# The last 512 queries of a transformer block's forward half in two chunks of 256, with the PSUM banks shared out anew

## Chip, cores and metric

One NeuronCore of a Trainium2 chip. The metric is device time in microseconds (us) of one launch. The engines are written PE (matrix products, "TensorE"), ACT (ScalarE), DVE (VectorE), POOL (GpSimd) and SP (which here only issues DMAs). Matrix products go into PSUM, eight banks of 128 partitions by 512 float32; a tile of 128x1024 float32 takes two banks.

## The reference, cut to what matters

A block of adaptive layer norm, attention with 32 heads of 16 channels, and a two-layer network with squared ReLU, over 2048 tokens of width 512. The kernel must give the block's output and its gradients by nine inputs.

```
mod = (_silu(c) @ w_mod).reshape(c.shape[0], 6, 1, -1)       # sa, ca, ga, sb, cb, gb
h = _layernorm(x) * (1 + ca) + sa
x = x + ga * _A_ref(h, A_wqkv, A_wo)                          # attention, S = 2048, H = 32, Dh = 16
h = _layernorm(x) * (1 + cb) + sb
x = x + gb * _B_ref(h, B_w1, B_b1, B_w2, B_b2)                # (relu(h @ w1 + b1)**2) @ w2 + b2, F = 1792
...
_out, _vjp = jax.vjp(_f, A_x, A_wqkv, A_wo, B_w1, B_b1, B_w2, B_b2, c, w_mod)
_grads = _vjp(grad_out)
```

## The kernel before, in words

There are four stages. A short preparation makes the first projections. The **forward** stage (`fscore`, `fpv`, lines 567 to 610) runs the attention. A stage **between** (`late_finish`, `last_chunk`, lines 650 to 668 and 1233 to 1490) does the dense work of the last queries. The **backward** stage (lines 1594 to 1760) runs the attention's gradient, and a tail makes the projections' gradients. The change touches the forward stage and the stage between.

**Forward.** The 2048 queries are four chunks of 512. The loop goes over 512 units (`funits`): for each chunk, for each of 8 groups of 4 heads, for each of 16 key tiles of 128 keys. One unit makes the scores of 4 heads (line 576: four PE products of 32 rows each, in four row groups of the array), two exponentials on ACT (line 578, each 128x1024 from a score tile of two banks), and, two units later, the products with the values (line 592: four products of 32 columns in four column groups, all into one bank `oacc`). PSUM holds three score tiles (six banks), `oacc`, and one bank `pm` for everything else.

**Dense work beside it.** When a chunk's 128 units are over, `ffinish` starts the generator `dense_chunk` for it: the output projection `wo`, the second layer norm, w1 (line 410), the first part of the gradient (w2 transposed, line 424), the products back through w1 (line 446), the network's output through w2 (line 500) and through `wo` transposed (line 532). It is advanced by `step` (line 1119), once a unit, beside the next chunk's attention; every `yield` ends a unit's share, most often four products of 512 columns. Each product lands in the one bank `pm` and is taken out by DVE. Weight gradients are "chains" (`add_chain`, line 226; the queue is `dwq`): four products, a copy by DVE into one of four `part` tiles (line 251), and a DMA that adds it to a partial sum in DRAM, issued on POOL's queue (line 255). A unit that makes no product of its own gets two idle products into `oacc` (`steady`, line 615), which add zero.

**Between.** The last chunk has no attention to hide under. After the last unit, `late_finish` completes its attention output, and `last_chunk` does its dense work alone, 512 queries at a time, with ACT and DVE sharing the evictions, the transposes on PE (line 1322), and the final sum of every weight gradient (line 237), for which the partial sums are fetched by SP's queue and the results stored by ACT's. The weights w1 (transposed) and w2 are loaded again for it, and the head rows, keys and gradients that the backward stage starts with come in as well (`head_loads`).

**Order.** All five engines stand in a hand-written order: an engine executes what the loops record, in that order, and waits in place. A recorded `later(k, ...)` is put out k units (in the stage between: k ticks) later, at the start of a unit.

## Time and profile before

| | |
|---|---|
| three runs | 2475.92, 2488.13, 2494.58 us; median 2488.13 |
| span of the profiled execution | 2501.3 us |
| first to last exponential of the forward stage | 41.2 to 996.3 us of the span |
| first exponential of the backward stage | 1115.66 us |
| exponentials of the forward stage (line 578) | 1024, 941.9 us busy |

The span is that of one execution under the profiler; it lies 13 us (0.5%) above the median of the three runs. Matmuls are pipelined in the array, so their time of about 0.38 us each overlaps with that of their neighbours; what counts for PE is how far apart they start. A group of instructions is written as engine, line, output<-inputs and shape; a tile's number is left out.

### The profile page before, as it was taken

How to read it: one execution, taken by the hardware profiler on the slowest of the kernel's cores; microseconds unless marked ns; L12 is line 12 of the kernel's file. 1: busy time of each engine (PE TensorE's matmuls, PEld its weight loads, DVE VectorE, ACT ScalarE, POOL GpSimd, SP SyncE). 2: the span in 40 equal slices, each digit the busy share in tenths (PEclk: the TensorE clock that was granted, in tenths of full speed). 3: DMA queues.
4: the chain of work that ended last, by engine and by line, in shares of the span. 5: the costliest groups of instructions: out<-in, count | busy, mean ns of one | idle time of the engine just before them, and what ended most of it. 6: DMA issues, size and time to landing. Idle time of an engine off the chain costs nothing.

```text
span 2501.3 us, 49888 instructions
## 1 busy us (share of the span) xinstructions
PE 2324.0 (93%) x18948; PEld 783.4 (31%) x19036; DVE 1837.7 (73%) x2377; ACT 2303.7 (92%) x3560; POOL 488.0 (20%) x661
## 2 busy tenths in 40 slices
PE   8899899989998998999999999999999999999989
PEld 3232233223332333443223323233232323332344
DVE  6555354455435444579989999999999999999965
ACT  7999999999998999539999999999999999999944
POOL 2111223323533453110111101111011110110100
PEclk9999999999998999999999999999999999999999
DMA  4468463258546865979999999999999999999984
GB/s 146 130 167 176 144 150 97 88 166 142 98 95 142 151 131 110 256 200 196 201 192 206 199 198 202 196 204 203 205 205 198 205 202 199 200 198 214 201 253 133
DMA packets 1189503, 437.70 MB, mean 175 GB/s; under 512 B 1065867, under 2 KB 1160521, under 8 KB 1188878
## 3 DMA queue, kind: packets, MB, share of 16 engines
q1 hardware_dynamic: 1152414, 389.35, 79.0%
q0 software_dynamic: 19872, 27.09, 6.5%
q10 hardware_dynamic: 16976, 18.07, 2.9%
q8 instruction: 149, 2.44, 0.4%
q14 instruction: 92, 0.75, 0.1%
HBM read 98.30 MB, written 70.80 MB: 68 GB/s over the span
## 4 chain that ended last, share of the span: by engine, by line
ACT 40%; PE 38%; issue 8%; DVE 7%; DMA 3%; SPq 1%; ACTq 1%; POOL 0%; DVEq 0%; another core or an unknown queue 0%; POOLq 0%
ACT E_u L1600 24%; ACT ET L578 12%; PE dqacc L1681 4%; PE psST L576 3%; PE psS_A L1594 3%; PE accVK L1654 2%; PE pm L233 2%; ACT dsT L1760 2%; PE psS_B L1594 2%; PE pdh L1858 2%; PE oacc L592 2%; PE psS_C L1594 2%; PE pwq L1892 2%; PE pm L500 2%; PE pm L410 2%
## 5 line engine op out<-in xcount | busy, mean ns | idle before, releaser
L1616 DVE TENSOR_TENSOR dS_u<-psD_u,E_u 128x1024 bf16<-128x1024 f32 x1024 | 1185.9, 1218 | 77.1 <-PE psD_u L1614 30.2
L578 ACT ACTIVATE ET<-psST 128x1024 bf16<-128x1024 f32 x1024 | 941.9, 1242 | 16.6 <-PE psST L576 16.3
L1600 ACT ACTIVATE E_u<-psS_A 128x512 bf16<-128x512 f32 x768 | 509.9, 664 | 10.8 <-PE psS_C L1594 8.5
L1600 ACT ACTIVATE E_u<-psS_B 128x512 bf16<-128x512 f32 x768 | 503.2, 655 | 10.8 <-DMA dsT<-dS_u 2.7
L1614 PE MATMUL psD_u<-iv,ido 32*128 32x512 bf16 x2048 | 409.1, 388 | 1.5 <-DVE dS_u L1616 1.3
L576 PE MATMUL psST<-qt_sb,kt_sb 32*128 32x512 bf16 x2048 | 313.8, 386 | 48.0 <-ACT ET L578 41.0
L1600 ACT ACTIVATE E_u<-psS_C 128x512 bf16<-128x512 f32 x512 | 334.3, 653 | 3.1 <-PE psS_B L1594 1.1
L1594 PE MATMUL psS_B<-ik,iq 32*128 32x512 bf16 x768 | 296.1, 386 | 11.7 <-ACT E_u L1600 4.4
L1594 PE MATMUL psS_A<-ik,iq 32*128 32x512 bf16 x768 | 294.5, 383 | 11.0 <-DVE dwlast L237 1.0
L1699 POOL TENSOR_TENSOR dQacc<-dQacc,dqtmp 128x512 f32<-128x512 f32 x64 | 81.2, 1268 | 858.8 <-ACT dqtmp L1694 797.4
L1594 PEld LDWEIGHTS <-iq 32*128 32x128 bf16 x2048 | 129.7, 91 | 313.9 <-issue 296.9
L1654 PE MATMUL accVK<-dS_u,qz 128*32 128x512 bf16 x2048 | 213.5, 388 | 0.5 <-PE psD_u L1614 0.2
L592 PE MATMUL oacc<-ET,vaug 128*32 128x512 bf16 x2048 | 207.0, 394 | 3.9 <-DVE ostage L596 3.9
L1663 PE MATMUL accVK<-E_u,dOs_tok 128*16 128x512 bf16 x2048 | 204.5, 388 | 0.0
L1594 PE MATMUL psS_C<-ik,iq 32*128 32x512 bf16 x512 | 194.2, 379 | 4.5
L576 PEld LDWEIGHTS <-kt_sb 32*128 32x128 bf16 x2048 | 84.3, 91 | 328.2 <-issue 306.5
L1681 PE MATMUL dqacc<-dsT,KS_tok 128*32 128x512 bf16 x2048 | 145.7, 382 | 18.8 <-DMA dsT<-dS_u 5.0
L1760 ACT ACTIVATE dsT<-ptT 128x1024 bf16<-128x1024 bf16 x128 | 144.1, 1126 | 13.1 <-PE ptT L1644 12.2
L251 DVE COPY part<-pm 128x512 f32<-128x512 f32 (+2 forms) x106 | 65.2, 615 | 121.9 <-PE pm L233 111.8
L1614 PEld LDWEIGHTS <-ido 32*128 32x128 bf16 x2048 | 105.2, 91 | 101.3 <-issue 94.9
L1654 PEld LDWEIGHTS <-qz 128*32 128x32 bf16 x2048 | 58.5, 94 | 178.0 <-issue 162.9
L1699 POOL TENSOR_TENSOR dQst<-dQacc,dqtmp 128x512 bf16<-128x512 f32 x32 | 40.6, 1270 | 266.1 <-ACT dqtmp L1694 266.1
(415 smaller groups left out, 2688.7 us busy)
## 6 DMA issues: line engine op xcount, KB each, us to landing
p_st<-part POOLq DMA_DIRECT2D x36, 256.0 KB, 4.6
kt_sb<-qkT_st POOLq DMA_DIRECT2D x124, 64.0 KB, 3.0
wA<-in_B_w_dram SPq DMA_DIRECT2D x28, 256.0 KB
wB<-w1T_st SPq DMA_DIRECT2D x21, 256.0 KB
wA<-w2T_st SPq DMA_DIRECT2D x21, 256.0 KB
wB<-in_B_w_dram SPq DMA_DIRECT2D x21, 256.0 KB
p_st<-part POOLq DMA_DIRECT2D x28, 192.0 KB, 4.6
p_st<-part SPq DMA_DIRECT2D x18, 256.0 KB
```

The source lines that it names most:

```text
L576: PE.matmul(ps[:, hi, :], kt_sb[r:r + 32, kt * P:(kt + 1) * P], qt_sb[r:r + 32, :], start=True, stop=True, tile_position=(r, 0))
L578: ACT.activation(ET[:, 2 * pair:2 * pair + 2, :], ps[:], AF.Exp, scale=SCALE)
L592: PE.matmul(oacc[32 * hq:32 * hq + 32, :], lhsT, ET[:, hq, :], start=(kt == 0), stop=(kt == TT - 1), tile_position=(0, 32 * hq), skip_grou ...
L1594: PE.matmul(psS[:], st["q"][r:r + 32, qt * P:(qt + 1) * P], st["k"][r:r + 32, kc * 512:kc * 512 + 512], start=True, stop=True, tile_positi ...
L1600: ACT.activation(bst[u][0][:, hq, :], sst.pop((u, hq))[:], AF.Exp, scale=SCALE)
L1614: PE.matmul(psD[:, hi, :], st["do"][r:r + 32, qt * P:(qt + 1) * P], st["v"][r:r + 32, kc * 512:kc * 512 + 512], start=True, stop=True, til ...
L1616: DVE.tensor_tensor(dS_u[:, 2 * pair:2 * pair + 2, :], psD[:], E_u[:, 2 * pair:2 * pair + 2, :], ALU.mult)
L1654: PE.matmul(cur["vk"][32 * hq:32 * hq + 32, :], hst[hg]["qz"][:, qt, hq, :], bst[u][1][:, hq, :], start=(qt == 0), stop=False, tile_positi ...
L1663: PE.matmul(acc[32 * hq:32 * hq + DH, :], dOs_tok[:, qt, (hg * 4 + hq) * DH:(hg * 4 + hq + 1) * DH], E_u[:, hq, :], start=False, stop=(qt ...
L1681: PE.matmul(acc[32 * hq:32 * hq + 32, :], KS_tok[:, kc * 4 + kt, h * DH:h * DH + 32], tT[:, :, hq * 4 + kt, :], start=(kt == 0), stop=(kt ...
L1699: POOL.tensor_tensor(dst2, dst, tmp[:], ALU.add)
L1760: ACT.activation(dst, pt[:], AF.Identity)
```

## The change

The queries are cut into five chunks: three of four tiles of 128 queries, and two of two tiles (`CH`). A unit of a short chunk covers two key tiles for 256 queries, so there are still 512 units and 1024 exponentials of the same size; its score and value products have 256 columns and are twice as many. The dense work of the fourth chunk (256 queries) now runs in `dense_chunk` under the fifth's attention; only the fifth's is left to `last_chunk`. In the last 128 units `step` is called twice a unit. The products through w1 and w2 of a short chunk are 256 wide, and a `yield` stands after every second of them.

PSUM is shared out anew: two score tiles (four banks), `oacc`, two banks `pm`, and one bank `pg` for the long sums of lines 446 and 500 (14 products each), between which chains can now run. In a unit the first pair's scores come first, then the value products of two units before, then the second pair's scores. `steady` is left out as well where the generator ran without a product. The last two head groups, before the last one, are finished after the loop. The loads of a head group's keys and queries (`fload`) stand 12 units ahead of the group, and 7 units ahead, two a unit, behind a short chunk's group of 8 units.

```diff
     TT = n // P
     QC = n // 512
     NS = -(-FC // 3)
+    CH = [(4 * i, 4) for i in range(QC - 1)] + [(TT - 4, 2), (TT - 2, 2)]
+    NC = len(CH)
...
             else:
                 POOL.tensor_tensor(racc[:, j, :], racc[:, j, :], src, ALU.add)
 
-        open_group = [False]
+        def group():
+            products[0] += 1
+            return pools["mm"].tile([P, 512], F32, name="pg", tag="pg", bufs=1)
+
...
                     acc = mm()
-                for ti in range(4):
-                    PE.matmul(acc[:, 0:w], lhs(ti), rhs(ti), start=(ti == 0), stop=(ti == 3))
-                if c == QC - 1:
+                nt = CH[c][1]
+                for ti in range(nt):
+                    PE.matmul(acc[:, 0:w], lhs(ti), rhs(ti), start=(ti == 0), stop=(ti == nt - 1))
+                if c == NC - 1:
                     late = idx >= FC + 4 * NS
...
+            ts = slice(t0, t0 + nt)
+            end = c == NC - 1
+            L = dict(begun)
+            begun.clear()
+            if not L:
+                L["w1"] = load_wA(w1_src, 6)
+                L["g"] = chunk_tile("g_c", "g_c", nt)
+                sp(L["g"], g_dram[:, ts, :])
+            if not end:
+                L["w1T"] = load_wB(w1T_st[:], 20) if nt == 4 else load_wB(w1T_st[:], 6, 0.5)
...
-            for ti in range(4):
-                later(5 + ti, scaled, ti)
+            for ti in range(nt):
+                later(5 + ti if nt == 4 else 1 + ti, scaled, ti)
                 later(24 + 2 * ti, sums, ti)
             return L
 
...
-            ts = slice(4 * c, 4 * c + 4)
+            t0, nt = CH[c]
+            W = nt * P
+            every = 4 // nt
+            ts = slice(t0, t0 + nt)
...
...
-                    PE.matmul(pz[:], w1_nat[:, ic, fc * P:(fc + 1) * P], h2T[:, :, ic, :],
+                    PE.matmul(pz[:, 0:W], w1_nat[:, ic, fc * P:(fc + 1) * P], h2T[:, :, ic, :],
                               start=(ic == 0), stop=(ic == DC - 1))
-                DVE.tensor_scalar(rT[:, fc, :], pz[:], b1col[:, fc:fc + 1], 0.0, ALU.add, ALU.max)
+                DVE.tensor_scalar(rT[:, fc, :], pz[:, 0:W], b1col[:, fc:fc + 1], 0.0, ALU.add, ALU.max)
                 DVE.tensor_tensor(sT[:, fc, :], rT[:, fc, :], rT[:, fc, :], ALU.mult)
                 if fc % 3 == 2 or fc == FC - 1:
                     f0 = fc // 3 * 3
                     to_tokens("s", sT, f0, fc + 1)
-                yield 0
+                if fc % every == every - 1:
+                    yield 0
...
             rest = []
-            for ti in range(4):
-                t = 4 * c + ti
-                pdh = mm()
+            for ti in range(nt):
+                t = t0 + ti
+                pdh = group()
                 for fc in range(FC):
                     PE.matmul(pdh[:], dzT[:, fc, ti * P:(ti + 1) * P], w1T[:, fc, :],
                               start=(fc == 0), stop=(fc == FC - 1))
                     if fc == 3 and rest:
                         rest.pop()()
...
-        funits = [(qc, hg, kt) for qc in range(QC) for hg in range(HG) for kt in range(TT)]
+            for ti in range(nt):
+                later(lag + more, sp, d_st[:, (t0 + ti) * P:(t0 + ti + 1) * P], dltT[H * ti:H * ti + H, :])
+
+        funits = [(ch, hg, j) for ch in range(NC) for hg in range(HG) for j in range(TT * CH[ch][1] // 4)]
+        first = {}
+        for u, (ch, hg, j) in enumerate(funits):
+            if j == 0 and u > 0:
+                short = CH[funits[u - 1][0]][1] < 4
+                first.setdefault(u - (7 if short else 12), []).append((ch, hg, 2 if short else 1))
...
-        def fscore(u):
-            qc, hg, kt = funits[u]
-            qt_sb, kt_sb = fh[qc, hg]
-            ET = ework.tile([P, 4, 512], BF, name="ET", tag="ET")
-            fe[u] = ET
-            for pair in range(2):
-                ps = pools["s"].tile([P, 2, 512], F32, name="psST", tag="psST")
+            fh[c, hg] = (qt_sb, kt_sb)
+
+        def fscore(u, pair):
+            c, hg, j = funits[u]
+            nk = 4 // CH[c][1]
+            W = 512 // nk
+            qt_sb, kt_sb = fh[c, hg]
+            if pair == 0:
+                fe[u] = ework.tile([P, 4, 512], BF, name="ET", tag="ET")
+            ET = fe[u]
+            ps = pools["s"].tile([P, 2, 512], F32, name="psST", tag="psST")
+            for k in range(nk):
+                kt = j * nk + k
                 for hi in range(2):
                     r = 32 * (2 * pair + hi)
-                    PE.matmul(ps[:, hi, :], kt_sb[r:r + 32, kt * P:(kt + 1) * P], qt_sb[r:r + 32, :],
+                    PE.matmul(ps[:, hi, k * W:(k + 1) * W], kt_sb[r:r + 32, kt * P:(kt + 1) * P], qt_sb[r:r + 32, 0:W],
                               start=True, stop=True, tile_position=(r, 0))
-                ACT.activation(ET[:, 2 * pair:2 * pair + 2, :], ps[:], AF.Exp, scale=SCALE)
+            ACT.activation(ET[:, 2 * pair:2 * pair + 2, :], ps[:], AF.Exp, scale=SCALE)
 
...
-            qc, hg, kt = funits[u]
-            if kt == 0:
+            c, hg, j = funits[u]
+            nt = CH[c][1]
+            nk = 4 // nt
+            W = nt * P
...
                 if hg == 0:
-                    fcur["rr"] = ework.tile([H, 512], F32, name="rrows", tag="rrows", bufs=1)
-                    fcur["ou"] = ework.tile([P, 4, HG, P], BF, name="O_un", tag="O_un", bufs=1)
+                    if CH[c - 1][1] == nt and nt == 2:
+                        fcur["rr"], fcur["ou"] = fcur["next"]
+                    else:
+                        rr = ework.tile([H, 512], F32, name="rrows", tag="rrows", bufs=1)
+                        ou = ework.tile([P, 4, HG, P], BF, name="O_un", tag="O_un", bufs=1)
+                        fcur["rr"], fcur["ou"] = rr[:, 0:W], ou[:, 0:nt]
+                        fcur["next"] = rr[:, 256:512], ou[:, 2:4]
             oacc = fcur["o"]
             ET = fe.pop(u)
-            for hq in range(4):
-                h = hg * 4 + hq
-                lhsT = vaug[:, kt].rearrange("p h c -> p (h c)")[:, h * (DH + 1):h * (DH + 1) + 32]
-                PE.matmul(oacc[32 * hq:32 * hq + 32, :], lhsT, ET[:, hq, :],
-                          start=(kt == 0), stop=(kt == TT - 1), tile_position=(0, 32 * hq), skip_group_check=True)
-            if kt == TT - 1:
-                ostage = ework.tile([P, 512], F32, name="ostage", tag="ostage", bufs=1)
-                DVE.tensor_copy(ostage[:], oacc[:])
-                obf = ework.tile([P, 512], BF, name="obf", tag="obf", bufs=2)
-                if u == NF - 1:
-                    fcur["last"] = ostage
-                    return
-                if hg == HG - 1:
...
-                    POOL.tensor_copy(obf[:], ostage[:])
+            for k in range(nk):
+                kt = j * nk + k
                 for hq in range(4):
                     h = hg * 4 + hq
-                    later(2, sp, fcur["rr"][h:h + 1, :], ostage[32 * hq + 16:32 * hq + 17, :])
-                later(3, sp, fcur["ou"][:, :, hg, :], obf[:], True)
+                    lhsT = vaug[:, kt].rearrange("p h c -> p (h c)")[:, h * (DH + 1):h * (DH + 1) + 32]
+                    PE.matmul(oacc[32 * hq:32 * hq + 32, 0:W], lhsT, ET[:, hq, k * W:(k + 1) * W],
+                              start=(kt == 0), stop=(kt == TT - 1), tile_position=(0, 32 * hq), skip_group_check=True)
+            if kt == TT - 1:
+                if c == NC - 1 and hg >= HG - 2:
+                    last = ework.tile([P, 256], F32, name="olast", tag="obf", bufs=2)
+                    DVE.tensor_copy(last[:], oacc[:, 0:W])
+                    fcur["last", hg - HG + 2] = last
...
 
         def step(u):
             nonlocal wait, turn
-            ripe = dwq and not open_group[0] and u >= dwq[0][0]
-            if wait > 0 or not dense:
-                wait = max(0, wait - 1)
+            ripe = dwq and u >= dwq[0][0]
+            if u < wait or not dense:
                 if ripe:
                     next_chain()
                 return
...
                 dense.pop(0)
                 run_due(True)
                 if not fqueue:
-                    loads["L"] = chunk_loads(QC - 1)
-            else:
-                wait = w
-
-        fqueue = list(range(QC - 1))
+                    loads["L"] = chunk_loads(NC - 1)
+            elif w > 0:
+                wait = u + w + 1
+
+        fqueue = list(range(NC - 1))
...
-            pools["s"] = ph2.enter_context(tc.tile_pool(name="psS", bufs=3, space=bass.MemoryType.PSUM))
+            pools["s"] = ph2.enter_context(tc.tile_pool(name="psS", bufs=2, space=bass.MemoryType.PSUM))
...
-            pools["mm"] = ph2.enter_context(tc.tile_pool(name="psM", bufs=1, space=bass.MemoryType.PSUM))
+            pools["mm"] = ph2.enter_context(tc.tile_pool(name="psM", bufs=2, space=bass.MemoryType.PSUM))
...
                 fh[0, 0] = (qts[0], kts[0])
                 for u in range(NF + 2):
                     unit[0] = u
                     run_due()
+                    count = products[0]
+                    fast = u >= NF - TT * HG
                     if u < NF:
-                        if funits[u][2] == 4 and u + TT < NF:
-                            fload(*funits[u + TT][0:2])
-                        fscore(u)
+                        for args in first.pop(u, ()):
+                            fload(*args)
+                        fscore(u, 0)
                     if 2 <= u:
                         fpv(u - 2)
+                    if u < NF:
+                        fscore(u, 1)
                     if u % 4 == 2 and u // 4 < len(stages):
                         later_stage(stages[u // 4])
                     if u % 4 == 0 and 18 <= u // 4 < 32:
                         turn_weights(u // 4 - 18)
-                    count, begun_group = products[0], open_group[0]
                     for f, args in plan.pop(u, ()):
                         f(*args)
+                    worked = len(dense) > 0 and u >= wait
                     if u < NF - 4:
-                        step(u)
+                        for _ in range(2 if fast else 1):
+                            step(u)
                     elif dwq and u >= NF - 2:
                         next_chain()
-                    if products[0] == count and not (begun_group or open_group[0]):
+                    if products[0] == count and not worked:
                         steady(u - 2)
-                    if u >= NF - 7 and "L" in loads and "O" not in loads["L"]:
+                    if u >= NF - 8 and "L" in loads and "O" not in loads["L"]:
                         early_finish()
                     if u == NF:
                         tiny = wk.tile([P, 1], F32, name="tiny", tag="tiny", bufs=1)
...
             ACT.activation(dst, onesf[:, 0:1].to_broadcast([P, n]), AF.Identity, scale=value)
 
         def last_chunk(O_c, L, w1T, w2T):
-            c = QC - 1
-            ts = slice(4 * c, 4 * c + 4)
+            c = NC - 1
+            t0, nt = CH[c]
```

The rest of the diff carries the number of tiles `nt` of a chunk through the tile shapes, loops and slices of `chunk_loads`, `dense_chunk`, `attn_grad`, `store_grad`, `early_finish`, `late_finish`, `ffinish` and `last_chunk` (whose layer norm is now done in one half instead of two), and moves hooks in `last_chunk` accordingly.

## Prediction

> **What bounds the kernel now.** I read the page first: busy time by slices, then the costliest groups.

> ```profile
> span 2501.3 us, 49888 instructions
> ...
> PE   8899899989998998999999999999999999999989
> ...
> ACT  7999999999998999539999999999999999999944
> ...
> L578 ACT ACTIVATE ET<-psST 128x1024 bf16<-128x1024 f32 x1024 | 941.9, 1242 | 16.6 <-PE psST L576 16.3
> ```

> ACT is full in the first 16 slices, the forward stage, apart from 16.3 us in which it waited for scores; then comes a hole, the stage between. 941.9 us over 1024 exponentials is 0.92 us each; ends follow each other at 0.917, so ACT's floor is 1.835 us a unit, 939.5 us in all. With the 16 idle that is the 955.1 us from 41.2 to 996.3. So the forward stage is bound by ACT, and PE's nines there say little. How much room PE has is read from its timeline, in units with a dense product:

> ```profile
> 876.29 0.40 PE L592 MATMUL oacc<-ET,vaug 128*32 128x512 bf16 x4
> 876.63 1.04 PE L424 MATMUL pm<-gfT,wA 128*128 128x512 bf16 x4
> 877.60 0.39 PE L576 MATMUL psST<-qt_sb,kt_sb 32*128 32x512 bf16 x4
> 877.92 0.40 PE L592 MATMUL oacc<-ET,vaug 128*32 128x512 bf16 x4
> 878.52 1.02 PE L424 MATMUL pm<-gfT,wA 128*128 128x512 bf16 x4 [0.20 <-DVE rT L427]
> 879.48 0.39 PE L576 MATMUL psST<-qt_sb,kt_sb 32*128 32x512 bf16 x4
> ```

> Four score products start together and cost as much as one: the next kind of product starts 0.32 us after them (877.60 to 877.92), the one behind the value products likewise 0.32 to 0.34 after those, and four dense products take 0.96 (878.52 to 879.48). That is 1.60 us of 1.835; the 0.2 wait for the single bank `pm` fits in too. From the starts in the trace: products of one kind follow each other at 0.215 us with 512 columns, 0.161 with 384, 0.108 with 256 and 0.055 with 128, and a change of kind (32-row, 32-column or full array) adds 0.10.

> Last, the stage between, 119.4 us from 996.3 to 1115.7, cut at its loops (head, w1, w2 transposed, the long sums, tail):

> ```profile
> core 0: us, PE busy (x) PEld busy (x) DVE busy (x) ACT busy (x) POOL busy (x), PEclk, DMA share, GB/s
> 996.30:1016.90 20.60, 15.75 (x93) 7.05 (x93) 13.92 (x34) 11.81 (x23) 7.41 (x9) 0.96 0.95 234
> 1016.90:1045.20 28.30, 26.40 (x158) 12.72 (x160) 13.35 (x27) 17.10 (x28) 1.70 (x2) 0.97 1.03 268
> 1045.20:1070.50 25.30, 24.72 (x168) 13.73 (x168) 16.67 (x42) 11.02 (x18) 2.96 (x15) 1.00 0.82 250
> 1070.50:1107.90 37.40, 37.24 (x193) 16.56 (x194) 30.40 (x71) 11.79 (x25) 0.00 (x0) 1.00 0.79 213
> 1107.90:1115.70 7.80, 6.69 (x30) 2.38 (x29) 4.84 (x9) 0.64 (x2) 0.48 (x1) 1.00 0.70 229
> ```

> PE is busy in 110.8 of the 119.4 us, so PE bounds this stage; but the DMA engines move 238 GB/s meanwhile, 28.4 MB.

> **The first 384 units.** With two score tiles the pairs are split: scores, values, scores, so a quad's 0.32 us is paid twice. A unit costs PE 0.95 us (0.315 + 0.32 + 0.315) before dense work. I counted the products of each unit in the order of the built program. 204 units carry four products of 512 columns: 0.95 + 0.96 = 1.91 us, above ACT's 1.835. The other 180 stay below (mean 0.52 dense, 1.47 us) and cost nothing while ACT covers them. Added: 204 x 0.075 = 15.3 us, 720 instead of 704.6.

> The change adds a wait: the second pair needs the tile that the previous unit's second exponential leaves, and behind it on PE stand the dense products and the next unit's first pair, for which ACT waits. By the rows a tile's round is 0.05 from the end of an exponential to the scores, 0.385 for these, 0.10 to ACT, and at least 1.02 for the exponential (its shortest), 1.56 us: shorter than 1.835, so two tiles suffice unless PE is late. The longest way round, over the dense products and both tiles, is 0.315 + 0.96 + 0.385 + 0.10 + 1.02 + 0.917 + 0.05 = 3.75 us for two units, 1.87 each: below PE's own 1.91. Ends for this part: 10 us if coupling is kinder, 25 if the added waits on DVE come on top.

> **The last 128 units.** Two steps a unit, and PE's fixed 0.95 remains (eight products of 256 columns in place of four of 512: same columns; that 256-wide products of one row group follow without a gap is taken from the 0.108 of the full array; a further 0.10 for each would be 0.3 a unit). Units 384 to 507, dense time with the switch: 41 units of 1.7 us or more, mean 1.82, so 2.77 each, 113.6 us; 29 of mean 1.46, 69.8; 18 of mean 1.00, 35.1; 36 under ACT's floor, 66.1. Sum 284.5 us against 124 x 1.835 = 227.5: 57 more. Here PE is the bound, and ACT idles. The dense work is what it was (the fourth chunk's half under attention is new: about 45 us of products), but two steps in one unit fill PE while other units have nothing ripe.

> **What else moves forward.** The fourth chunk's four weight loads (7.3 MB), 38 chains (8.4 MB to add) and 32 more key loads of 64 KB (2.1 MB) join a stretch that moves 134 GB/s over 248 us (33.3 MB); 51 MB over some 320 us are 160 GB/s, below the 200 of the backward stage: hidden. POOL gains 8 groups x 9 loads x 0.55 us and 38 chains x 0.88, 73 us beside 103 busy of 248: hidden, but chains stand in its queue behind key loads. Chains themselves can stall: a `part` tile is busy for the copy (0.62), the issue (0.87) and the landing (4.6), 6.1 us, so four tiles serve a chain each 1.5 us. Before, one chain came a unit; a stall of this kind is in the trace all the same, 3.35 us at 768 where the copy waited for that DMA. Now some 15 units have two chains in 2.3 to 2.8 us: 0.3 to 0.8 us each, 6 us. The waits for DVE at chunk starts, most of the 16 us idle before, partly vanish with the second bank and partly stand in the open now: 10. Forward: 720 + 284.5 + 7.3 (the last four units) + 16 = 1028, against 955: **+73**, from +50 (these stalls gone, coupling kind) to +95 (256-wide products dearer, chains slower).

> **The stage between**, with half the queries: the head loses the second norm half (3.95 us, from 1009.40 to 1013.35), half of the four 0.5 us copies and of the first products, and its chains: 20.6 to 13. The w1 loop needs PE 12.8 us (56 x 0.108, 28 x 0.055, 24 x 0.215) instead of 26.4, but it moved 7.6 MB, which at its 268 GB/s takes 28 us and at the 422 GB/s that the trace's best 5 us show, 18: I take 18. The w2 loop likewise 11.5 on PE, 6.3 MB: 17. The long sums halve to 19, plus about 5 as finish, turn and gradient of a tile have fewer products to hide under: 24. The tail, with head loads that now come due at its end: 10. Sum 82, with a little for PE's half clock after gaps 84: **-35**. Bounds: PE and latencies alone 65 (-54); all 27.5 MB at 268 GB/s 103 (-16).

> The backward stage and tail are untouched. **Sum:** 2501.3 + 73 - 35 = 2539 us for a span like this one; on the median of the runs 2488.1 + 38 = 2526.

> [...]

> **Rivals.** (1) PE absorbs the second step: if products of two queued steps ran closer than 0.215 us, the excess of PE's sums would fall from 72 us to 28 at 0.16 and 13 at 0.13; with the stalls in ACT's shade forward stays at its 955 to 965, the stage between gives 35, and the time is 2458. It decides below about 0.14 us, where the sum's 17 and the stalls' 16 balance the 35. Against it: every row. [...] 6%; faster. (2) DMA bounds the stage between: it holds the same 34 final chains, weights and head loads in less time; at 268 GB/s it stays near 103 us, -16, so 2545. For it: a share of 0.95 to 1.03 in its first half. 17%. (3) The chains' ring and POOL's queue hold DVE, and DVE holds PE, through the last 128 units: another 25 us, 2551. For it: the stall at 768. Against: POOL would be busy in half of the time. 11%. (4) The small loss: forward +50, between near PE's floor, -50: 2488. 6%. That the fourth chunk's work is not done when the loop ends would undo the change, but in the built order its last chain stands in unit 510.

> **How the numbers follow.** The forecast (60%) is 2526, its own range 2500 to 2555 from the two sums' ends. 1% is about what a measurement can tell here (three runs spread by 0.75%), so slower means above 2513. Slower: 0.6 x 0.78 + 0.17 + 0.11 = 0.75. Within 1%: 0.6 x 0.22 + 0.06 = 0.19. Faster: rival 1, 0.06. The range, 2480 to 2580, takes in 2 to 4 with some microseconds for their own ends, and leaves out rival 1 and the far end of 3.

> **What would show it.** Right: exponentials evenly 1.83 us a unit in units without four dense products and about 1.91 with them, so 715 to 730 us for the first 384 units; 290 to 320 us from unit 384 to the last exponential, ACT idle for 60 us there, ended by `psST`; 75 to 100 us between last exponential and first `E_u`. Wrong: ACT full to the end of the forward stage (rival 1); DMA share above 1 all through the stage between (2); DVE waiting for `p_st` beyond 15 us (3); a backward stage that changes length, for which I have no term.

## The result, and the profile after

The changed kernel takes 2696.73 us (median of 4 runs, 2677.26 to 2721.0) against 2487.85 (4 runs, 2475.92 to 2494.58): a ratio of 1.0816, 95% interval 1.0753 to 1.0879. The ratio leaves out the run of 2721.0 us, which lies 1.6% above the fastest and counts as a slow one. It is slower, as forecast, but by 209 us in place of 38, and outside the range of 2480 to 2580.

The page of the profile after, its span, its slices and the group of the exponentials:

```profile
span 2697.6 us, 52498 instructions
...
PE   8899999999998898788699999999999999999989
...
ACT  7999768998998666565399999999999999999954
...
PEclk9999558998988799877799999999999999999999
...
L620 ACT ACTIVATE ET<-psST 128x1024 bf16<-128x1024 f32 x1024 | 986.3, 1034 | 204.0 <-PE psST L618 201.5
```

ACT now waits 201.5 us for scores (16.3 before). The third line, PEclk, is the granted clock: the share of its full clock that PE had in each slice, in tenths. The same line of the page before has a single slice below 9:

```profile
PEclk9999999999998999999999999999999999999999
```

In the changed kernel, in slices 5 and 6, PE has its nines, its granted clock is 0.5, and ACT falls to 7 and 6. In slices 12 to 14 and 17 to 18, the later part of the forward stage, the clock is at 7 or 8 again (a slice is 67 us).

Cut as the prediction cut it, from the first exponential at 42.8 us (41.2 before), with the time that the clock stood at half rate in brackets:

| us | before | predicted | after |
|---|---|---|---|
| units 0 to 383 | 707.1 (10) | 720 | 803.4 (208) |
| units 384 to 507 | 239.6 (14) | 284.5 | 374.4 (119) |
| last four units | 8.4 (0) | 7.3 | 9.1 (9) |
| stalls, as a term of its own | | 16 | (in the rows above) |
| forward stage | 955.0 (24) | 1028 | 1186.9 (336) |
| stage between | 119.4 (3) | 84 | 97.9 (33) |
| backward stage and tail | 1385.7 (70) | as before | 1370.0 (40) |

So 159 us of the error lie in the forward stage and 14 in the stage between; the backward stage and tail took 16 back. The stage between after, at the same loops (head, w1, w2 transposed, long sums, tail); columns as before:

```profile
1229.70:1242.80 13.10, 8.12 (x43) 3.25 (x42) 7.71 (x19) 5.53 (x9) 0.00 (x0) 0.76 0.85 291
1242.80:1265.60 22.80, 17.07 (x104) 9.18 (x106) 12.79 (x29) 13.04 (x28) 0.00 (x0) 0.87 0.75 233
1265.60:1282.50 16.90, 14.28 (x113) 9.78 (x111) 12.10 (x40) 5.29 (x14) 2.50 (x14) 0.91 0.93 292
1282.50:1310.10 27.60, 22.43 (x101) 9.31 (x103) 17.40 (x40) 8.95 (x17) 0.54 (x3) 0.88 0.73 212
1310.10:1327.60 17.50, 3.49 (x16) 1.29 (x17) 4.71 (x8) 0.38 (x1) 0.00 (x0) 0.68 0.86 254
```

PE no longer bounds it (its idle time is 32.5 of 97.9 us), and the clock in the seventh column is below 1 in every loop.

**Where the first 384 units lost it.** PE's timeline of the changed kernel around 258.4 us, where the clock falls, in units without dense products (L618 scores of a pair, L644 values, L670 the idle products that add zeros):

```profile
256.46 0.39 PE L618 MATMUL psST<-qt_sb,kt_sb 32*128 32x512 bf16 x2 [0.53 <-ACT ET L620]
256.78 0.40 PE L644 MATMUL oacc<-ET,vaug 128*32 128x512 bf16 x4
257.38 0.39 PE L618 MATMUL psST<-qt_sb,kt_sb 32*128 32x512 bf16 x2 [0.20 <-ACT ET L620]
257.70 0.60 PE L670 MATMUL oacc<-identb,zeros 128*16 128x512 bf16 x2
258.30 0.53 PE L618 MATMUL psST<-qt_sb,kt_sb 32*128 32x512 bf16 x2
258.76 0.62 PE L644 MATMUL oacc<-ET,vaug 128*32 128x512 bf16 x4
259.31 0.61 PE L618 MATMUL psST<-qt_sb,kt_sb 32*128 32x512 bf16 x2
259.84 1.02 PE L670 MATMUL oacc<-identb,zeros 128*16 128x512 bf16 x2
260.80 0.60 PE L618 MATMUL psST<-qt_sb,kt_sb 32*128 32x512 bf16 x2
```

Up to 258.3 a pair's scores reach the next step in 0.32 us, behind it in 0.54, and from one unit's first pair to the next (258.30 to 260.80) it is 2.50 us in place of ACT's 1.83. No bracket follows: PE waits for nothing. It stays so for 163.8 us, units 114 to 173. The kernel before falls at the same place (250.6 us, at a unit without idle products), and there too PE needs more than 1.83 for a unit with idle products at half clock, 2.38 us from scores to scores:

```profile
251.34 1.05 PE L576 MATMUL psST<-qt_sb,kt_sb 32*128 32x512 bf16 x4
...
253.72 0.54 PE L576 MATMUL psST<-qt_sb,kt_sb 32*128 32x512 bf16 x4
```

But it is back after 3.4 us, and its exponentials go on ending 1.83 or 1.84 us a unit apart: PE had been ahead, waiting 0.20 to 0.53 us for ACT to free a score tile (246.3 to 250.0 us), and the lead lasted. What differs is how long the clock stays down.

### The profile page after: what moved, and what is told of

It reads as the page before. It is cut to its first block, busy times and chain, and to the rows that moved or that the text cites. A ratio compares the mean times of both kernels' runs of the same rounds, so it can differ in the third digit from the quotient of the medians.

```text
span 2697.6 us, 52498 instructions
## 1 busy us (share of the span) xinstructions
PE 2494.6 (92%) x19977; PEld 833.5 (31%) x20074; DVE 1880.9 (70%) x2512; ACT 2326.5 (86%) x3535; POOL 572.2 (21%) x805
## 4 chain that ended last, share of the span: by engine, by line
ACT 43%; PE 37%; DMA 6%; issue 6%; DVE 4%; POOL 1%; ACTq 1%; SPq 1%; DVEq 0%; POOLq 0%
ACT E_u L1648 22%; ACT ET L620 17%; PE psST L618 6%; PE dqacc L1729 4%; PE oacc L644 3%; PE psS_A L1642 3%; PE accVK L1702 2%; ACT dsT L1808 2%; PE pm L433 2%; PE psS_B L1642 2%; DMA dsT<-dS_u 2%; PE pg L523 2%; PE psS_C L1642 2%; PE pdh L1906 2%; PE pm L239 2%
## 5 line engine op out<-in xcount | busy, mean ns | idle before, releaser
L620 ACT ACTIVATE ET<-psST 128x1024 bf16<-128x1024 f32 x1024 | 986.3, 1034 | 204.0 <-PE psST L618 201.5
L618 PE MATMUL psST<-qt_sb,kt_sb 32*128 32x512 bf16 (+1 forms) x2560 | 447.5, 377 | 45.4 <-ACT ET L620 29.5
L618 PEld LDWEIGHTS <-kt_sb 32*128 32x128 bf16 x2560 | 118.8, 94 | 397.7 <-issue 384.8
L644 PE MATMUL oacc<-ET,vaug 128*32 128x512 bf16 (+1 forms) x2560 | 229.5, 385 | 10.7 <-DVE ostage L653 10.7
L257 DVE COPY part<-pm 128x512 f32<-128x512 f32 (+2 forms) x152 | 91.3, 606 | 194.8 <-PE pm L239 145.9
L261 POOL DMA_DIRECT2D p_st<-part x114 | 107.0, 1030 | 152.3 <-DVE part L257 148.3
```

The costliest lines, as they stand in the source:

```text
L261: POOL.dma_start(out=p_st[idx][:, 0:w], in_=part, accum_op=ALU.add)
L618: PE.matmul(ps[:, hi, k * W:(k + 1) * W], kt_sb[r:r + 32, kt * P:(kt + 1) * P], qt_sb[r:r + 32, 0:W], start=True, stop=True, tile_position ...
L620: ACT.activation(ET[:, 2 * pair:2 * pair + 2, :], ps[:], AF.Exp, scale=SCALE)
L644: PE.matmul(oacc[32 * hq:32 * hq + 32, 0:W], lhsT, ET[:, hq, k * W:(k + 1) * W], start=(kt == 0), stop=(kt == TT - 1), tile_position=(0, 3 ...
```

## The experiments

The theories. **Clock**: split pairs leave the array less work, the clock falls to half rate, and a unit that then needs more than ACT's 1.835 us keeps it there. **Work and waits**: the doubled steps need more of PE, of the chains' ring (the four `part` tiles, used in turn) and of the weights than the sums say. Runs are one execution each, unless said; the kernel before took 2479.8 to 2496.9 us on the same chips.

**e1, three idle products and the old condition for them**, in the changed kernel:

```
-                for _ in range(2):
+                for _ in range(3):
...
-                    if products[0] == count and not worked:
+                    if products[0] == count and not (begun_group or open_group[0]):
```

> The changed kernel with three idle products (into oacc, adding zero) instead of two in every unit in which no product runs, and also in the units where the changed kernel leaves them out because the generator ran without a product. Theory 'clock': the array's clock falls to half for 336 us of the forward stage because units with split pairs and few products leave the array too little to do; three idle products keep it up. Then half clock in the forward stage under 100 us, units 128 to 255 back from 291 to about 245 us, the time 2590 to 2630 us. Rival 'work': the loss is PE's added work and its waits, and the low clock only follows from them; a third idle product is more work, and the time is 2690 to 2730 us, units 128 to 255 near 290 us.

Measured 2660.43 us, between the two expectations. The fall at unit 114 is gone; the first 384 units take 757.2 us with 44 at half clock. Units 384 to 507 did not gain: 383.4, 121 at half clock. Idle products reach only the first part. How much they gain there is not settled by one execution: e5 and e12 below run the same code in these units and took 758.7 and 790.1 us, with 41 and 120 at half clock.

**e2, the split alone**: the kernel before with two score tiles and the new order of a unit (first pair, values, second pair); chunks, steps and dense banks as before.

```
-                        fscore(u)
+                        fscore(u, 0)
                     if 2 <= u:
                         fpv(u - 2)
+                    if u < NF:
+                        fscore(u, 1)
...
-            pools["s"] = ...(name="psS", bufs=3, ...)
+            pools["s"] = ...(name="psS", bufs=2, ...)
```

> The kernel before with one part of the change alone: two score tiles instead of three, and the second pair's scores behind the value products. Chunks, dense work and the single bank for it as before. Theory 'clock': the split pairs alone bring the half clock, over 100 us of it in the forward stage (24 before), most of it where no dense work runs, units 112 to 175; the time 2540 to 2590 us. Rival 'work', the term of the prediction: 0.075 us in each unit with four dense products, 15 us for the first 384 units and 5 for the rest, half clock as before: 2500 to 2515 us.

Measured 2604.5 us, above even the first expectation: the split with its two tiles costs some 110 alone. The first 384 units take 799.9 us, 181 at half clock, close to the changed kernel (803.4, 208), and the fall at unit 114 lasts 75 us. With one step a unit, units 384 to 507 take 259.8, 20 more than before.

**e3, the chunks and doubled steps alone**: the changed kernel with the score tiles, the quads (all four scores of a unit together), the single dense bank and the old condition for idle products of before.

```
-            pools["s"] = ...(name="psS", bufs=2, ...)
+            pools["s"] = ...(name="psS", bufs=3, ...)
...
-            pools["mm"] = ...(name="psM", bufs=2, ...)
+            pools["mm"] = ...(name="psM", bufs=1, ...)
...
                         fscore(u, 0)
+                        fscore(u, 1)
                     if 2 <= u:
                         fpv(u - 2)
-                    if u < NF:
-                        fscore(u, 1)
```

> The other part alone: the five chunks, two steps a unit in the last 128 units, with PSUM as before (three score tiles, all four scores together, one bank for every dense product). Theory 'clock': with the scores in one piece the array stays at full clock (under 60 us at half in the forward stage), the first 384 units take 707 us as before, the last 128 about 300 to 330 with the single bank's waits, the stage between about 98 instead of 119: 2520 to 2570 us. Rival 'work': the last 128 units take 360 us and more as in the changed kernel, because two steps a unit are what costs: 2580 us or more.

Measured 2638.59 us (4 runs), a ratio of 1.0575 (1.0522 to 1.0628), as the rival had it. The first 384 units are those of before, 709.5 us with 14 at half clock. All of the loss is in units 384 to 507: 404.1 us. So e2 and e3 part the loss by place: the split acts mainly in the first 384 units, the doubled steps in units 384 to 507. PE's longest wait there in e3 is that for the single bank:

```profile
PE pm L240 <- DVE part L258: 41.3, 35, 5.6
```

**e5, e1 without the adding DMAs of two chunks' chains**:

```
-                else:
+                elif c < QC - 2:
                     POOL.dma_start(out=p_st[idx][:, 0:w], in_=part, accum_op=ALU.add)
```

> e1_warm3 without the DMAs that add the weight-gradient parts of the third and fourth chunk to DRAM; the weight gradients of these chunks are left out of the outputs. Theory 'ring': four part tiles that each wait for copy, issue and landing (6 us) hold DVE, and DVE holds PE, in the last 128 units; without the DMAs these units are 30 to 50 us shorter than in e1_warm3. Rival 'work': PE's products set the pace, the part tiles cost under 12 us.

Measured 2636.18 us. Units 384 to 507 take 359.8 us, 23.6 less than in e1 (between the two expectations), and PE's idle time there falls from 65 to 43 us: about that much hangs on the landing of these DMAs, that is, on the time until their data is written. The half clock there stays at 106 us.

**e6, e1 with idle products of 32 rows**:

```
-PE.matmul(fcur["o"][0:DH, 0:nt * P], zeros[:], identb.unsqueeze(1).to_broadcast([P, nt, P]), start=False,
+PE.matmul(fcur["o"][0:DH, 0:nt * P], zeros[0:32, :], identb[0:32].unsqueeze(1).to_broadcast([32, nt, P]), start=False,
...
```

> The kernel of e1_warm3 (three idle products in a unit without other products), whose idle products now use 32 rows of the array in place of 128, at the same 512 columns; they add zeros, so nothing computed changes. If the clock follows how much of the array works, the half clock in the first 384 units rises from 44 us to above 150 and the span from 2659 to 2690 to 2740. If it follows only whether PE is busy, the half clock stays at 30 to 80 us and the span at 2640 to 2675.

Measured 2847.98 us, the way of the first expectation and far beyond it, 188 more than e1, with the same count and columns of products; at half clock the three idle ones lengthen a unit to 3.00 us in both. The first 384 units take 942 us, 512 of them at half clock. PE and then ACT in the longest stretch, 225 us from 679.5:

```profile
734.77 0.61 PE L624 MATMUL psST<-qt_sb,kt_sb 32*128 32x512 bf16 x2
735.31 0.62 PE L650 MATMUL oacc<-ET,vaug 128*32 128x512 bf16 x4
735.86 0.61 PE L624 MATMUL psST<-qt_sb,kt_sb 32*128 32x512 bf16 x2
736.40 1.89 PE L435 MATMUL pm<-h2T,wA 128*128 128x512 bf16 x4
738.22 0.61 PE L624 MATMUL psST<-qt_sb,kt_sb 32*128 32x512 bf16 x2
```

```profile
735.48 2.06 ACT L626 ACTIVATE ET<-psST 128x1024 bf16<-128x1024 f32 x2 [1.40 <-PE psST L624]
738.92 2.05 ACT L626 ACTIVATE ET<-psST 128x1024 bf16<-128x1024 f32 x2 [1.39 <-PE psST L624]
```

A unit with four dense products takes 3.45 us, at half clock, with PE idle nowhere in these lines and for 2.6 us in the whole stretch. In the 3.4 us before this stretch PE was idle for 0.05. So in this run PE was busy, and yet the clock fell and stayed at half. What the edit took away is rows, 32 for 128 in the idle products, and the first 384 units went from 44 us at half clock (e1) to 512. (This is one execution, but 512 us lie far outside the 7 to 120 of the five with 128 rows, e1, e5, e12, e13 and e14.)

**e7, the changed kernel with idle products over 128 output columns**:

```
-PE.matmul(fcur["o"][0:DH, 0:nt * P], zeros[:], identb.unsqueeze(1).to_broadcast([P, nt, P]), start=False,
+PE.matmul(fcur["o"][:, 0:nt * P], identb[:], zeros[:, 0:1].to_broadcast([P, nt * P]), start=False,
...
```

> The changed kernel with its own two idle products a unit and its own condition, each of them over 128 output columns of the array (identity as weights, zeros moving) in place of 16; nothing computed changes. If output columns count for the clock, the half clock in the first 384 units falls from 208 us to below 80 and the span from 2698 to 2615 to 2650. If they do not count, 150 to 260 us at half clock and a span of 2675 to 2720.

Measured 2695.49 us, as the second expectation had it and that of the changed kernel; 174 us at half clock in the first 384 units against 208. The output columns show no effect that is larger than the difference between executions of one kernel.

**e8, the kernel before without its idle products**:

```
-                for _ in range(2):
+                for _ in range(0):
```

> The kernel before without its idle products (quads and three score tiles as they were); nothing computed changes. If the clock needs them, the half clock of the forward stage rises from 24 us to above 120; a unit with four dense products then needs 0.53 + 0.53 + 1.8 = 2.9 us at half clock instead of 1.835, so the span is 2530 to 2620. If quads keep the clock up by themselves, at most 60 us at half clock and a span of 2485 to 2510. In both cases its backward stage, which is that of the kernel before, shows how far that stage varies between executions: 1246 to 1262 us.

Measured 2503.44 us. Half of the expectation failed: the clock falls as said (201 us of the forward stage, one stretch of 109), but it costs only 10.7 us of that stage (965.7). PE and ACT at half clock:

```profile
202.86 9.54 ACT L578 ACTIVATE ET<-psST 128x1024 bf16<-128x1024 f32 x10
203.81 0.62 PE L592 MATMUL oacc<-ET,vaug 128*32 128x512 bf16 x4
204.35 0.61 PE L1065 MATMUL ptk<-identb,KT 128*128 128x128 bf16 x4
204.89 0.81 PE L576 MATMUL psST<-qt_sb,kt_sb 32*128 32x512 bf16 x4
...
205.64 0.62 PE L592 MATMUL oacc<-ET,vaug 128*32 128x512 bf16 x4
```

The unit (203.81 to 205.64) fits into 0.54 + 0.54 + 0.75 = 1.83 us even so, and ACT has no gap. In these runs half clock costs time where PE's sum at half clock exceeds ACT's 1.835 for longer than PE's lead lasts; the split pairs, at 0.54 + 0.54 + 0.55 before anything dense or idle (e6, above), leave 0.2 us of room, and two idle products take 0.96 (259.84 to 260.80 in the changed kernel).

**e11, the changed kernel without idle products**:

```
-                for _ in range(2):
+                for _ in range(0):
```

> The changed kernel without its idle products; nothing computed changes. In its trace a unit with idle products took 2.58 us at half clock, of which 0.97 are the idle products themselves; without them such a unit needs 1.6 and ACT's 1.83 set it, while a unit with four dense products still needs 3.45. If the idle products cost more at half clock than they keep up, the first 384 units take 740 to 790 us (803 with them) and the span is 2630 to 2685. If they are what brings the clock back, there are over 350 us at half clock in these units, which then take 830 to 950 us, and the span is 2720 to 2850.

Measured 2688.86 us, between the two expectations: 280 us at half clock in the first 384 units, which take 793.5 (803.4 with them). The 54 units with nothing beside scores and values at half clock now take 1.88 us in the mean, near ACT's floor; in the changed kernel 28 units with two idle products took 2.55. But more units with dense products are at half clock, 58 in place of 35. With split pairs the two idle products cost about what they gain.

Its trace also shows best how the last 124 units lose time. Timeline behind 852 us, a few lines of it:

```profile
854.02 0.42 DVE L257 COPY part<-pm 128x256 f32<-128x256 f32 x1 [7.56 <-DMA p_st<-part]
854.50 1.01 PE L239 MATMUL pm<-tk,h_c 128*128 128x256 bf16 x4 [6.41 <-DVE part L257]
...
855.44 0.60 PE L618 MATMUL psST<-qt_sb,kt_sb 32*128 32x256 bf16 x4
...
856.15 3.88 ACT L620 ACTIVATE ET<-psST 128x1024 bf16<-128x1024 f32 x4 [6.68 <-PE psST L618]
```

DVE's copy waits 7.56 us for a tile of the ring, PE 6.41 for that copy, ACT 6.68 for PE; from 852.1 the clock is at half for 27 us (scores 0.60). In the changed kernel, PE idled for 1.0 to 2.9 us of the 3.4 us before each of the eight falls after unit 384.

**e12, e1 without the chains of the third and the fourth chunk**:

```
             def run():
+                if QC - 2 <= c < NC - 1:
+                    return
```

> The kernel of e1_warm3 without the weight-gradient chains of the third and the fourth chunk: their products, the copies of the sums, and the adding DMAs are left out (weight gradients lack these chunks). At full clock the products of units 384 to 507 then sum to 267 us with ACT's floor, against 284.5 with the chains. If the chains (copies on DVE that wait for a tile of the ring, and PE behind them) make the stalls there, these units fall from 383 us to 285 to 305 and the half clock in them from 122 us to below 60. If the stalls are those of loads and chunk starts, with the clock behind them, they stay at 335 to 370.

Measured 2639.22 us. Units 384 to 507 in e1 and then in e12 (stretch, PE, weight loads, DVE, ACT, POOL busy, clock, DMA share, GB/s):

```profile
800.00:1183.40 383.40, 318.16 (x2796) 124.22 (x2822) 195.10 (x424) 241.23 (x249) 196.27 (x298) 0.84 0.77 149
```

```profile
832.70:1166.40 333.70, 293.96 (x2695) 113.24 (x2692) 152.19 (x349) 240.40 (x250) 131.69 (x225) 0.83 0.53 122
```

49.7 us less, of which the sums gave 17.5, and at the edge of the second expectation. (The whole kernel gains only 21 us on e1, because its first 384 units, with e1's code, took 33 more.) PE's idle time falls from 65.2 to 39.7 us. The sums hold 28.3 of these 39.7 under ACT's floor, and 16.7 of the 65.2, so the idling that they do not hold falls from 48.5 to 11.4: the chains make most of it. But the clock stays at 0.83, and PE is busy 294 us with products that sum to 239 at full clock. The clock accounts for that: four dense products take 0.96 us at full clock (878.52 to 879.48 in the kernel before) and 1.82 at half (736.40 to 738.22 in e6), nearly twice as long. PE was busy for 102.5 us at half clock here, and half of it, 51 us, is nearly the difference.

**e13, e1 with the key and query loads of the last two chunks on SP; e14, besides a longer lead for the second weights**:

```
-                later(i // rate, POOL.dma_start, to, fro)
+                later(i // rate, sp if c >= QC - 1 else POOL.dma_start, to, fro)
...
-            yield 3
+            yield 3 if c < QC - 2 else 6
```

> The kernel of e1_warm3, whose key and query loads for the last two chunks are issued by SP instead of POOL; nothing computed changes. In its trace DVE's copies waited 44.6 us for an adding DMA to free a tile of the ring in the last 128 units, and these DMAs stood behind such loads in POOL's queue. If POOL's queue makes those waits, they fall below 20 us and units 384 to 507 from 383 to 345 to 372. If it is the landing itself, or if SP's weight loads now come late in exchange, the units stay at 375 to 400.

> The kernel of e13_loads_sp, which besides waits six units in place of three between the first and the second product loop of the third and the fourth chunk, so that the second weights have landed (PE waited 10.4 us for them in e1_warm3); nothing computed changes. If each gap on PE costs itself and some 3 us more at half clock behind it, units 384 to 507 fall by another 8 to 15 us against e13_loads_sp. If the six units only move the work later, they stay within 5 us of it.

e13 measured 2661.4 us, e14 2635.58. Units 384 to 507: 370.1 and 373.4 us. In e13 DVE's waits for the ring fall from 45.9 to 31.8, less than expected, and PE has a new wait of 9.2 us for `wo_nat` on SP; the longer lead in e14 takes PE's wait for the second weights from 4.9 to 1.0 us and gains nothing, and the ring's waits are back at 40.7. What e14 gained over e13 is not the edit: up to unit 372, where the first loads go to SP, both run e1's code, and in the first 384 units e1, e13 and e14 had 44, 37 and 7 us at half clock and took 757.2, 754.3 and 742.3 us (e5 and e12: 41 and 120, 758.7 and 790.1). These windows of the first 384 units, of the changed kernel and then of e14, hold the price of the clock:

```profile
42.80:846.20 803.40, 763.17 (x4435) 230.56 (x4485) 345.92 (x689) 736.68 (x769) 207.32 (x342) 0.87 0.49 116
```

```profile
42.70:785.00 742.30, 709.54 (x4564) 236.07 (x4614) 348.26 (x689) 728.83 (x769) 203.75 (x333) 1.00 0.53 126
```

More products in e14, less time, at a clock of 1.00. None of the variants of the changed kernel comes near the one before. A longer ring for `part` was not tried.

## Why the prediction was wrong

**The step that failed** is the unit sum of the forward stage, "204 units carry four products of 512 columns: 0.95 + 0.96 = 1.91 us", "2.77 each" and the rest: every term took the spacing at full clock, and half clock was allowed for only in the stage between ("a little for PE's half clock after gaps"). The trace of before had 24 us of half clock in its forward stage, in stretches of 3.4 and 6.8 us, and they cost next to nothing there; the prediction put them at nothing after the change too, without a reason. By parts:

- *First 384 units*, 83 us off. Nearly free of half clock they take 742 us (e14), of which 6 are e14's third idle product (units 49 to 101: 105.3 us, 99.4 in the changed kernel). So at full clock the split costs some 736 us, not 720: a unit with four products came out at 1.94 us, not 1.91, and lighter ones too were up to 1.94. That is a mis-sized term: it adds some 29 us to before's 707, where the sum had 15 and an end of 25. The other 67 or so are the clock (803.4 - 736). The changed kernel's own units agree: its 81 units that are at half clock, wholly or in part, took 75 us more than 1.835 each. e2 shows that the split with two tiles brings the half clock, 181 us in place of 10; e6, that with idle products of 32 rows it falls and stays down (512 us in place of e1's 44); e8, that with quads it may fall with little loss (201 us at half clock in the forward stage, for 10.7 us). Why split pairs keep it down for longer is not shown.
- *Two tiles suffice*: right at full clock. PE waited 24.9 us for score tiles in the first 384 units, 0.8 at most, and units without products kept ACT's 1.83. Whether a third tile's lead would have bridged the falls, no run shows: every kernel with split pairs has two.
- *Units 384 to 507*, 90 us off. The price of a full unit was right: units at full clock with some 1.7 us or more of dense work took 2.80 us in the median, against 2.77. By the windows PE was idle 60.8 us of the 374.4, where the sums hold 16.7, and busy 313.6, where they hold 267.8: **44 us of waits** and **46 us of slower products**, the clock: PE was busy for 89.5 us at half clock in these units, and half of that is 45. Of the waits the chains make most (e12), the landing of their DMAs nearly half (e5). The sum had 16 us for all stalls.
- *"Hidden"* was argued by shares. DMA moved 152 GB/s in these units, and POOL was busy 195.9 of 374.4 us, both near what was foreseen. What decided was order: one late landing stopped DVE, then PE, then ACT (7.56, 6.41 and 6.68 us in e11, at 854 to 856 us).
- *Stage between*, -21.5 in place of -35. The head (13.1 for 13) and the w2 loop (16.9 for 17) came as worked out; w1 22.8 for 18, the sums 27.6 for 24, the tail 17.5 for 10. In the tail ACT waits for `d_st`, which was in no term:

```profile
ACT E_u L1648 <- DMA d_st<-dltT: 16.5, 1, 16.5
PE psS_A L1642 <- ACT E_u L1648: 12.0, 1, 12.0
```

- *Backward stage and tail untouched*: right, though they were 15.7 us shorter. e2 and e8 have before's own backward stage and took 1246.3 and 1251.8 us there against 1260.6 in the profile of before; the kernels with the changed one 1245.5 to 1259.8. The profiled execution of before was a long one, as its span, 13 us above its median, said.

**The rivals.** PE absorbs the second step: no, ACT idles. DMA bounds the stage between: the time (97.9) lies near its 103, but the shares are 0.73 to 0.93 and none above 1; the clock, below 1 in every loop, and `d_st` are what the traces show in its place. Ring and POOL's queue: real. DVE waited 40.1 us for `p_st` in units 384 to 507, above the 15 named as its mark, and e5 and e12 put the price at 24 and 32 us (49.7 less the 17.5 of the products), near the 25 given to it; with 11% it was held too unlikely. No rival had the clock, which cost some 110 us (67 and 46).

What stays open: how the 46 us of slower products part between falls behind a wait and falls in light units, since no run held the clock up in the last units; why split pairs with two tiles have longer falls than quads with three, and which of the two matters; and what ends a stretch at half clock.

## What to carry to other kernels

A span bound by ACT can hide what PE's clock does (in e8, 201 us of the forward stage at half clock cost 10.7 us), so read the granted clock even where PE is not the bound. Before PE's room is spent, work the unit out a second time with the spacing at half clock: where it exceeded ACT's floor here, 2.50 us against 1.83 in the changed kernel, time was lost for as long as the clock stayed down, 163.8 us. And look at a ring of tiles that is emptied by DMAs in the order of the copying engine and of all who wait for it: here DVE's copies waited 40.1 us for it in 21 waits, up to 6.5 at a time, while POOL, whose queue issues these DMAs, was busy for 195.9 of 374.4 us.
